# FNet mixing and a squared-ReLU FFN on one core: three of eight P-Q products of a block made on VectorE

## The chip, the cores and the metric

The kernel runs on one core of one Trainium2 chip. The metric is the device time of one execution in microseconds. The engines are named as in the profile: PE is TensorE's matmul stream and PEld its weight loads, DVE is VectorE, ACT is ScalarE, POOL is GpSimd, SP is SyncE, which here only issues transfers.

## The reference

The input x is 8 x 3008 x 256. It is Fourier-transformed along the sequence and along the features; the real part goes through a feed-forward layer without biases.

```python
X = np.fft.fft(x, axis=1)
X = np.fft.fft(X, axis=2)
h = np.maximum(X.real.reshape(24064, 256) @ w_in, 0.0)   # w_in 256 x 2048
out = (h * h @ w_out).astype(np.float32)                 # w_out 2048 x 256
```

## The kernel before, in words

**The algebra.** The real part at frequency k is a cosine product plus a sine product, and at -k it is the same cosine product minus the sine product. So only half of the frequencies are carried. For each of them the kernel holds two vectors over features, zc and zs, as fp16 columns with the features on the partitions. The feature transform is folded into the first weight: gh (three versions of w_in, 128 folded features by 2048) has the cosine weight in gh[0], the sine weight in gh[1], and in gh[2] minus two times the sine weight. Row 0 of zs is an exception: it carries the Nyquist feature, which has the same sign at k and -k, and row 0 of gh[2] is therefore zero. With P = gh[0]·zc and Q = gh[1]·zs the hidden value at k is P+Q, and at -k it is P-Q but for the Nyquist term, which stays.

**The units.** For each of the 8 batches VectorE folds x into sums and differences (`fold_steps`, L312 on: `d_even`, `n_cos`, `d_odd`, `n_sin`, `odds`, `nyq`, `even`), and PE multiplies the folded data with cosine and sine tables in two units per batch (`z_steps`). A unit has 12 or 18 matmuls of 376 or 377 columns into a PSUM tile pz. ACT copies the first half's product to es (L408) and the whole sum to zc or zs (L412); VectorE makes the mirrored columns as 2·es - pz (`minus`, L419). `d_odd` also issues the loads of the next batch's x on POOL (`load_x`, one direct and two indexed transfers, L118 and L123).

**The blocks.** All 12040 columns of zc and zs are cut into 25 windows, which the change's title calls blocks: 240, 512, 512, 240, then twenty of 512, and a last one of 296. A window has eight steps (`NST`), each for 256 of the 2048 hidden features, in a PSUM tile ph of two banks, one bank for each half (a = 0, 1) of 128 features. There are two such tiles (`ps_h`). A step does, in the order written:

- `pq(s)`: four matmuls, P+Q for the two halves (L570, L571);
- `square(s, 0)`: ACT's relu of both halves from PSUM to fp16 (L580), and VectorE's square of that into h2 (L582);
- `others(s)`: a share of the other work: fold jobs, two jobs of the second GEMM of the window before (sixteen matmuls of 256 columns, L500; in every second step also ACT's copy of the result, L506, and SP's stores, L482), and a share of the z matmuls for the next window;
- `turn(s)`: two matmuls with gh[2] on the same banks (L576), which turn P+Q into P-Q;
- `square(s, 1)`: relu and square again, columns reversed, into the second half of h2.

Every engine executes its instructions in the order in which the program writes them, and the framework inserts the waits. The folds of a batch are placed in one window, two ahead of the window in which the batch's first unit begins: one job in each of steps 0 to 4, `nyq` in step 5, `even` in step 6 (`fold_at`, `fold_jobs`). The z jobs of a unit are spread over the eight steps of the window ahead of the one in which its first column lies; the last job of the cosine half, with its L412 and L419, falls into step 5, that of the sine half into step 7.

Of the kernel before, what the change touches and what calls it, by code (L numbers as in the profile page):

```python
# [8 lines left out]
F32 = mybir.dt.float32  # L9
F16 = mybir.dt.float16  # L10
I32 = mybir.dt.int32
AF = mybir.ActivationFunctionType
ALU = mybir.AluOpType

HS = 32.0
P = 128
# [3 lines left out]
def rev_dim(ap, i):  # L20

    dims = [list(d) for d in ap.ap]
    step, cnt = dims[i]
    dims[i] = [-step, cnt]
    return bass.AP(tensor=ap.tensor, offset=ap.offset + step * (cnt - 1), ap=dims)
# [3 lines left out]
def kernel(  # L29
# [12 lines left out]
    nc = tc.nc  # L42
# [7 lines left out]
    NFC = F // P  # L50
    WN = 512
# [7 lines left out]
    NE = 2 * (E // 2) + 1  # L59
# [7 lines left out]
    wins = []  # L67
    g = 0
    while g < TOT:
        n = min(FIRST[len(wins)] if len(wins) < len(FIRST) else WN, TOT - g)  # L70
        wins.append((g, n))
        g += n
    NW = len(wins)

    def win_of(col):
        return max(w for w in range(NW) if wins[w][0] <= col) if col < TOT else NW
# [5 lines left out]
    col_of = {}  # L82
# [11 lines left out]
    const = ctx.enter_context(tc.tile_pool(name="const", bufs=1))  # L94
    tmp = ctx.enter_context(tc.tile_pool(name="tmp", bufs=2))
# [7 lines left out]
    ps_h = ctx.enter_context(tc.tile_pool(name="ps_h", bufs=2, space=bass.MemoryType.PSUM))  # L103
    ps_o = ctx.enter_context(tc.tile_pool(name="ps_o", bufs=2, space=bass.MemoryType.PSUM))
# [66 lines left out]
    def small(shape, name):  # L171
        return const.tile(shape, F32, name=name)
# [95 lines left out]
    dvec = small([P, 2], "dvec")  # L268
# [5 lines left out]
    at = const.tile([P, 2, P + 1], F32, name="at")  # L274
# [85 lines left out]

    gh = const.tile([P, 3, F], F16, name="gh")

    def gh_step(cc):
        f0 = cc * 512
        pg = ps_h.tile([P, 2, 512], F32, name="pg", tag="psh")
        for i, t in enumerate((c_all, s_n)):
            for c in range(2):
                nc.tensor.matmul(pg[:, i, :], t[:, c, 0:P], w16[:, c, f0 : f0 + 512], start=(c == 0), stop=(c == 1))  # L368
        nc.scalar.activation(gh[:, 0:2, f0 : f0 + 512], pg, AF.Copy, bias=0.0, scale=1.0 / HS)  # L369
# [7 lines left out]
    def zwin(w):  # L377
        if w not in zc:
            zc[w] = zp.tile([P, WN], F16, name="zc", tag="zc")
            zs[w] = zp.tile([P, WN], F16, name="zs", tag="zs")  # L380
        return zc[w], zs[w]
# [64 lines left out]
    run(*z0(0, 0))  # L446
    run(f0s["d_odd"])
    gh_step(0)
    run(*z0(0, 1))
    run(f0s["n_sin"], lambda: f0s["odd"](1), f0s["nyq"])  # L450
    gh_step(1)
    gh_step(2)
    run(*z0(1, 0))
    run(*z0(1, 1))
# [31 lines left out]
    def ffn2_steps(w, h2):  # L486

        g0, wn = wins[w]
        groups = [(q, min(P, 2 * wn - q)) for q in range(0, 2 * wn, P)]
        jobs = []  # L490
        st = {}

        def part(i, hf):
            q, m = groups[i]
            j = i % 2
            if j == 0 and hf == 0:
                st["po"] = ps_o.tile([P, 512], F32, name="po", tag="po")
            po = st["po"]
            for fc in range(hf * 8, hf * 8 + 8):
                nc.tensor.matmul(po[0:m, j * D : (j + 1) * D], h2[:, fc, q : q + m], wout16[:, fc, :], start=(fc == 0), stop=(fc == NFC - 1))  # L500
            if hf == 1 and (j == 1 or i + 1 == len(groups)):
                osb = osp.tile([P, 2, D], F32, name="osb", tag="osb")
                for a, b in ((i - j, i),) if j == 0 or m == P else ((i - 1, i - 1), (i, i)):
                    mm = groups[b][1]
                    lo, hi = (a % 2) * D, (b % 2 + 1) * D
                    nc.scalar.activation(osb[0:mm].rearrange("p s d -> p (s d)")[:, lo:hi], po[0:mm, lo:hi], AF.Copy, bias=0.0, scale=HS * HS)  # L506
                for b in range(i - j, i + 1):
                    q1, m1 = groups[b]
                    nu = max(0, min(m1, wn - q1))
                    if nu:  # L510
                        store(osb[:, b % 2, :], 0, g0 + q1, nu, False)
                    if nu < m1:
                        store(osb[:, b % 2, :], nu, g0 + 2 * wn - q1 - m1, m1 - nu, True)

        for i in range(len(groups)):
            for hf in range(2):
                jobs.append(lambda i=i, hf=hf: part(i, hf))
        return jobs

    def spread(jobs, i, n):  # L520
        return jobs[len(jobs) * i // n : len(jobs) * (i + 1) // n]

    def fold_jobs(i):
        f = fold_steps(i)
        return [f["d_even"], f["n_cos"], f["d_odd"], f["n_sin"], f["odds"], f["nyq"], f["even"]]

    fold_at = {}
    for i in range(2, B):
        fold_at[win_of(col_of[i, 0]) - 2] = i
    NST = NFC // 2  # L530
    old = None
    for w in range(NW):
        g0, wn = wins[w]
        h2 = h2p.tile([P, NFC, 2 * WN], F16, name="h2", tag="h2")
        zcw, zsw = zwin(w)

        lo = 0
        at = [[] for _ in range(NST)]
        post = [[] for _ in range(NST)]
        if w == 0:  # L540
            at[2] = [f0s["even"]]
        elif w == 1:
            fj = fold_jobs(1)
            at = [[f] for f in fj[0:5]] + [[], fj[6:7], []]
            post[5] = fj[5:6]
            lo = 6
        elif w == 2:
            te = table_steps(1)
            at = [[lambda: te["freq"](), lambda: te["args"](0)], [], [lambda: te["turns"](0)], [], [lambda: te["mods"](0)],
                  [lambda: te["absm"](0)], [lambda: te["sins"](0)], [lambda: te["coss"](0)]]  # L550
        elif w == 3:
            at = [[lambda: te["args"](1)], [lambda: te["turns"](1)], [lambda: te["mods"](1)],
                  [lambda: te["absm"](1), lambda: te["sins"](1)], [lambda: te["coss"](1)], [lambda: te["weigh"]()], [], []]
            lo = 6
        elif w in fold_at:
            fj = fold_jobs(fold_at[w])
            at = [[f] for f in fj[0:5]] + [[], fj[6:7], []]
            post[5] = fj[5:6]
        zj, zl = [], []
        for u in need[w + 1]:  # L560
            zu = z_steps(u)
            zj += [(zu, 0, 0), (zu, 1, 0), (zu, 0, 1), (zu, 1, 1)]
        f2 = ffn2_steps(*old) if old else []
        phs = {}

        def pq(s):
            ph = phs[s] = ps_h.tile([P, 2, 512], F32, name="ph", tag="psh")
            for a in range(2):
                f0 = (2 * s + a) * P
                nc.tensor.matmul(ph[:, a, 0:wn], gh[:, 0, f0 : f0 + P], zcw[:, 0:wn], start=True, stop=False)  # L570
                nc.tensor.matmul(ph[:, a, 0:wn], gh[:, 1, f0 : f0 + P], zsw[:, 0:wn], start=False, stop=True)  # L571

        def turn(s):
            for a in range(2):
                f0 = (2 * s + a) * P
                nc.tensor.matmul(phs[s][:, a, 0:wn], gh[:, 2, f0 : f0 + P], zsw[:, 0:wn], start=False, stop=True, skip_group_check=True)  # L576

        def square(s, sg):
            h1 = h1p.tile([P, 2, 512], F16, name="h1", tag="h1")
            nc.scalar.activation(h1[:, :, 0:wn], phs[s][:, :, 0:wn], AF.Relu)  # L580
            hv = rev_dim(h1[:, :, 0:wn], 2) if sg else h1[:, :, 0:wn]
            nc.vector.tensor_tensor(h2[:, 2 * s : 2 * s + 2, sg * wn : (sg + 1) * wn], hv, hv, op=ALU.mult)  # L582

        def others(s):
            for j in at[s]:
                j()
            for j in spread(f2, s, NST):
                j()
            for j in post[s]:
                j()  # L590
            if s == lo:
                zl[:] = [j for zu, part, h in zj for j in zu(part, h)]
            if s >= lo:
                for j in spread(zl, s - lo, NST - lo):
                    j()

        ng = 2 if w == 0 else 1
        for s0 in range(0, NST, ng):
            ss = range(s0, s0 + ng)
            for s in ss:  # L600
                pq(s)
            for s in ss:
                square(s, 0)
            for s in ss:
                others(s)
            for s in ss:
                turn(s)
            for s in ss:
                square(s, 1)
        old = (w, h2)  # L610
    for j in ffn2_steps(*old):
        j()
# [30 lines left out]
```

## Time and profile before

| what | value |
|---|---|
| median of 3 runs | 650.95 us (650.9 to 651.0) |
| the profiled execution's own time | 650.93 us |
| its span in the profile | 649.2 us |
| granted TensorE clock | 1.0 |
| ACT relu, 128 x 1024 | 352, mean 1026 ns |
| DVE square, 128 x 1024 | 352, mean 692 ns |
| PE matmuls of L576 with 512 columns | 352, mean 379 ns |
| DVE busy in eight stretches of 22 to 27 us in the middle | 10.3 to 17.7 us |

The profile is of one execution. The time of the execution is the span and 1.7 us around it, so sums are made against 650.93. A matmul's duration runs from its start to its modelled end, and matmuls overlap: 379 ns is the life of one, while the next starts 0.215 us later. Likewise two neighbouring instructions of ACT or DVE overlap by about 0.1 us, so the sum of the busy times is a little more than the time taken.

### The profile page before, as it was taken

Reading aid. Unit: us, or ns where it says so; the run is one execution under the profiler, and the core shown is the slowest. Engines: PE = TensorE matmul, PEld = TensorE weight load, DVE = VectorE, ACT = ScalarE, POOL = GpSimd, SP = SyncE. Lnnn points to the kernel's source line nnn. Section 1 sums busy time; section 2 is a strip of 40 time slices with the busy share of each in tenths; the row PEclk is TensorE's granted clock in tenths of the full one; section 3 lists DMA queues with packets and bytes.
Section 4 is the critical chain, followed back from the end, with each engine's and each line's share of the span. In section 5 each row is a group of like instructions: output and inputs, shape, how many; then the busy total and the mean of one; then the engine's idle time right before and its main releaser. Section 6 shows DMA issues by size and latency. Waiting matters only on the chain.

```text
span 649.2 us, 11358 instructions
## 1 busy us (share of the span) xinstructions
PE 628.7 (97%) x4524; PEld 442.1 (68%) x4524; DVE 359.9 (55%) x580; ACT 462.4 (71%) x616; POOL 38.1 (6%) x59
## 2 busy tenths in 40 slices
PE   3789999999999999999999999999999999999997
PEld 1456786667677666776667676766767667766786
DVE  8786566744475445644466454764547544444431
ACT  7877867776777777677667777777766777677662
POOL 6120000200010000100002000020000000000000
PEclk9999999999999999999999999999999999999999
DMA  8924120611152111611116111171111111111112
GB/s 161 163 43 102 33 66 18 129 49 28 42 114 77 33 50 33 124 57 50 33 49 130 42 41 48 36 135 45 49 34 49 33 49 35 41 41 46 38 49 71
DMA packets 34085, 40.06 MB, mean 62 GB/s; under 512 B 3568, under 2 KB 29680, under 8 KB 34032
## 3 DMA queue, kind: packets, MB, share of 16 engines
q1 hardware_dynamic: 27136, 24.65, 13.1%
q0 software_dynamic: 6896, 14.69, 13.0%
q8 instruction: 35, 0.57, 0.4%
q14 instruction: 18, 0.15, 0.1%
HBM read 29.37 MB, written 24.64 MB: 83 GB/s over the span
## 4 chain that ended last, share of the span: by engine, by line
PE 91%; ACT 4%; DMA 2%; issue 2%; DVE 1%; POOL 1%; ACTq 0%; POOLq 0%
PE po L500 49%; PE ph L571 12%; PE ph L576 12%; PE ph L570 12%; PE pz L403 5%; ACT h L580 2%; DMA w<-in_moe_w_in_dram 2%; ACT gh L369 1%; ACT osb L506 0%; POOL xo L123 0%; ACT zs L412 0%; PE pg L368 0%; DVE h L582 0%; DVE zs L419 0%; ACT cos L252 0%
## 5 line engine op out<-in xcount | busy, mean ns | idle before, releaser
L580 ACT ACTIVATE h<-ph 128x1024 f16<-128x1024 f32 (+2 forms) x400 | 368.9, 975 | 107.6 <-PE ph L576 104.7
L582 DVE TENSOR_TENSOR h<-h 128x1024 f16<-128x1024 f16 (+2 forms) x400 | 262.7, 660 | 247.1 <-ACT h L580 245.3
L500 PE MATMUL po<-wout,h 128*128 128x256 f16 (+1 forms) x3024 | 361.7, 273 | 0.0
L500 PEld LDWEIGHTS <-h 128*128 128x128 f16 (+1 forms) x3024 | 296.5, 98 | 71.5
L570 PE MATMUL ph<-zc,gh 128*128 128x512 f16 (+2 forms) x400 | 145.2, 366 | 1.2 <-ACT gh L369 0.7
L571 PE MATMUL ph<-zs,gh 128*128 128x512 f16 (+2 forms) x400 | 145.2, 366 | 1.1 <-DVE zs L419 0.9
L576 PE MATMUL ph<-zs,gh 128*128 128x512 f16 (+2 forms) x400 | 113.8, 366 | 3.2 <-ACT h L580 2.9
L506 ACT ACTIVATE osb<-po 128x512 f32<-128x512 f32 (+3 forms) x97 | 56.6, 587 | 67.0 <-PE po L500 63.6
L571 PEld LDWEIGHTS <-gh 128*128 128x128 f16 x400 | 39.0, 98 | 45.0 <-issue 2.8
L570 PEld LDWEIGHTS <-gh 128*128 128x128 f16 x400 | 39.0, 97 | 44.8 <-issue 3.7
L576 PEld LDWEIGHTS <-gh 128*128 128x128 f16 x400 | 39.0, 98 | 20.4 <-issue 6.3
L118 POOL DMA_DIRECT2D xo<-in_x_dram x8 | 6.1, 761 | 272.0 <-DVE fo L331 272.0
L123 POOL DMA_INDIRECT xo<-in_x_dram,idx_r x15 | 18.4, 1224 | 4.5 <-issue 4.3
L408 ACT ACTIVATE es<-pz 128x376 f32<-128x376 f32 (+1 forms) x32 | 15.4, 482 | 4.0 <-PE pz L403 4.0
L419 DVE SCALAR_TENSOR_TENSOR zs<-es,pz 128x376 f16<-128x376 f32 (+22 forms) x27 | 9.5, 384 | 15.6 <-ACT zs L412 15.6
L419 DVE SCALAR_TENSOR_TENSOR zc<-es,pz 128x376 f16<-128x376 f32 (+22 forms) x27 | 9.5, 384 | 13.0 <-ACT zc L412 13.0
L327 DVE TENSOR_TENSOR fe<-xo 128x3072 f16<-128x3072 f16 x8 | 14.3, 1786 | 0.3
L331 DVE TENSOR_TENSOR fo<-xo 128x3072 f16<-128x3072 f16 x8 | 14.2, 1778 | 0.0
L297 PE MATMUL pw<-spc 128*128 128x384 f16 x28 | 6.3, 395 | 8.2 <-DVE spc L293 8.2
L403 PE MATMUL pz<-cos,od 128*128 128x376 f16 x48 | 12.2, 323 | 1.8 <-DVE od L343 1.8
L403 PE MATMUL pz<-sin,od 128*128 128x376 f16 x48 | 12.2, 322 | 1.1 <-ACT es L408 1.1
L403 PEld LDWEIGHTS <-od 128*128 128x128 f16 x96 | 9.3, 98 | 5.5 <-DVE od L343 2.1
(88 smaller groups left out, 174.3 us busy)
## 6 DMA issues: line engine op xcount, KB each, us to landing
out_dram<-osb SPq DMA_DIRECT2D x93, 128.0 KB
xo<-in_x_dram POOLq DMA_DIRECT2D x7, 768.0 KB, 7.5
w<-in_moe_w_in_dram POOLq DMA_DIRECT2D x1, 1024.0 KB, 12.0
wout<-in_moe_w_out_dram POOLq DMA_DIRECT2D x1, 1024.0 KB, 16.4
out_dram<-osb SPq DMA_DIRECT2D x5, 120.0 KB
out_dram<-osb SPq DMA_DIRECT2D x4, 115.0 KB
out_dram<-osb SPq DMA_DIRECT2D x5, 80.0 KB
xo<-in_x_dram POOLq DMA_DIRECT2D x1, 384.0 KB, 4.8
```

The lines of the kernel that those rows point to most:

```text
L123: nc.gpsimd.indirect_dma_start(out=flat(q), out_offset=None, in_=bass.AP(tensor=x.tensor, offset=0, ap=[[XW, B * S * D // XW], [1, XW]]), ...
L327: nc.vector.tensor_tensor(fef[:, :, 1:129], lo, hi, op=ALU.add)
L403: nc.tensor.matmul(ps[:, 0:n], lhs, tab, start=(h == 0 and k == 0), stop=last, skip_group_check=True)
L408: nc.scalar.activation(es[:, 0:n], ps[:, 0:n], AF.Copy, bias=0.0, scale=1.0)
L419: nc.vector.scalar_tensor_tensor(out=zwin(w)[part][:, o : o + cnt], in0=es[:, a : a + cnt], scalar=2.0, in1=ps[:, a : a + cnt], op0=ALU.mu ...
L500: nc.tensor.matmul(po[0:m, j * D : (j + 1) * D], h2[:, fc, q : q + m], wout16[:, fc, :], start=(fc == 0), stop=(fc == NFC - 1))
L506: nc.scalar.activation(osb[0:mm].rearrange("p s d -> p (s d)")[:, lo:hi], po[0:mm, lo:hi], AF.Copy, bias=0.0, scale=HS * HS)
L570: nc.tensor.matmul(ph[:, a, 0:wn], gh[:, 0, f0 : f0 + P], zcw[:, 0:wn], start=True, stop=False)
L571: nc.tensor.matmul(ph[:, a, 0:wn], gh[:, 1, f0 : f0 + P], zsw[:, 0:wn], start=False, stop=True)
L576: nc.tensor.matmul(phs[s][:, a, 0:wn], gh[:, 2, f0 : f0 + P], zsw[:, 0:wn], start=False, stop=True, skip_group_check=True)
L580: nc.scalar.activation(h1[:, :, 0:wn], phs[s][:, :, 0:wn], AF.Relu)
L582: nc.vector.tensor_tensor(h2[:, 2 * s : 2 * s + 2, sg * wn : (sg + 1) * wn], hv, hv, op=ALU.mult)
```

## The change

Blocks from number 5 on that are 512 columns wide get another order in their steps 2, 4 and 6 (`second_kind`). There the two matmuls of `turn` are not made. Instead:

- `first(s)` multiplies P alone; for each half VectorE makes P' = P + wny·zny into an fp32 tile in SBUF, where zny is row 0 of zs on all 128 partitions and wny the Nyquist weight of each hidden feature;
- after `others(s)`, `second(s)` adds Q to the same banks;
- ACT makes the relu of P+Q, VectorE makes 2P' - (P+Q) in fp16 (`minus`), and VectorE squares the first relu;
- the relu of the second value, by ACT in place in SBUF, and its square are put off (`later`) into the next step, behind that step's first relu and square.

In the plain steps of all blocks but the first the square of P-Q is also put off, behind the next step's P', where that step is a changed one. zny is made by one transfer on SP's queue at the start of each such block, which reads row 0 of zs 128 times. wny is made once, in block 3 (`wny_step`: one small VectorE operation, sixteen matmuls of one column, a copy). The folds of batches 3 to 7 are spread over three blocks, begin four ahead of the batch's first unit, and stand in steps 0, 1 and 7 alone. That gives 57 changed steps in 19 blocks.

```diff
+    def wny_step():
+        nc.vector.tensor_scalar(out=e0, in0=dvec[:, 0:1], scalar1=0.0, scalar2=None, op0=ALU.is_equal)
+        pn = ps_o.tile([P, 512], F32, name="pn", tag="po")
+        for fc in range(NFC):
+            nc.tensor.matmul(pn[:, fc : fc + 1], gh[:, 1, fc * P : (fc + 1) * P], e0, start=True, stop=True)
+        nc.vector.tensor_copy(wny, pn[:, 0:NFC])
...
-        fold_at[win_of(col_of[i, 0]) - 2] = i
+        w1 = win_of(col_of[i, 0])
+        if i == 2:
+            fold_at[w1 - 2] = (i, [(0, 0), (1, 1), (2, 2), (3, 3), (4, 4), (5, 5), (6, 6)])
+        else:
+            fold_at[w1 - 4] = (i, [(0, 0), (1, 7)])
+            fold_at[w1 - 3] = (i, [(2, 0), (3, 7)])
+            fold_at[w1 - 2] = (i, [(4, 0), (5, 1), (6, 7)])
+    def second_kind(w):
+        if w < 5 or wins[w][1] < WN:
+            return ()
+        return (2, 4, 6)
...
+        def first(s):
+            ph = phs[s] = ps_h.tile([P, 2, 512], F32, name="ph", tag="psh")
+            pt = tmp.tile([P, 3, NE], F32, name="pt", tag="tt")...
+            for a in range(2):
+                f0 = (2 * s + a) * P
+                nc.tensor.matmul(ph[:, a, 0:wn], gh[:, 0, f0 : f0 + P], zcw[:, 0:wn], start=True, stop=True)
+            for a in range(2):
+                nc.vector.scalar_tensor_tensor(out=pt[:, a, 0:wn], in0=zny[:, 0:wn], scalar=wny[:, 2 * s + a : 2 * s + a + 1], in1=ph[:, a, 0:wn], op0=ALU.mult, op1=ALU.add)
+            return pt
+        def second(s):
+            for a in range(2):
+                f0 = (2 * s + a) * P
+                nc.tensor.matmul(phs[s][:, a, 0:wn], gh[:, 1, f0 : f0 + P], zsw[:, 0:wn], start=False, stop=True, skip_group_check=True)
+        def minus(s, pt):
+            vv = tmp.tile([P, 3, NE], F32, name="vv", tag="tm")...
+            nc.vector.scalar_tensor_tensor(out=vv[:, :, 0:wn], in0=pt[:, :, 0:wn], scalar=2.0, in1=phs[s][:, :, 0:wn], op0=ALU.mult, op1=ALU.subtract)
+            return vv
+        def relu_v(vv, wn=wn):
+            nc.scalar.activation(vv[:, :, 0:wn], vv[:, :, 0:wn], AF.Relu)
...
+        kinds = second_kind(w)
+        if kinds:
+            zny = tmp.tile([P, NE], F32, name="zny", tag="kf")[:, 0 : WN // 2].bitcast(F16)
+            z1 = zsw[0:1, 0:wn]
+            nc.sync.dma_start(out=zny[:, 0:wn], in_=bass.AP(tensor=z1.tensor, offset=z1.offset, ap=[list(z1.ap[0]), [0, P], [1, wn]]))
...
+                if s in kinds:
+                    pt = first(s)
+                    while later:
+                        later.pop(0)()
+                    others(s)
+                    second(s)
+                    h1 = relu(s, 0)
+                    vv = minus(s, pt)
+                    square(s, 0, h1)
+                    later += [lambda vv=vv, f=relu_v: f(vv), lambda s=s, vv=vv, f=square: f(s, 1, vv)]
+                else:
+                    pq(s)
+                    square(s, 0, relu(s, 0))
+                    while later:
+                        later.pop(0)()
+                    others(s)
+                    turn(s)
+                    h1 = relu(s, 1)
+                    later.append(lambda s=s, h1=h1, f=square: f(s, 1, h1))
+                    if s + 1 not in kinds:
+                        later.pop(0)()
```

More of the change, by code (lines that the diff above doesn't have):

```diff
@@ L361 @@
     gh = const.tile([P, 3, F], F16, name="gh")
+    wny = small([P, NFC], "wny")
+    e0 = const.tile([P, 1], F16, name="e0")
+    def wny_step():
[4 more added lines that the diff above has]
+        nc.vector.tensor_copy(wny, pn[:, 0:NFC])
     def gh_step(cc):
@@ L525, in fold_jobs @@
         return [f["d_even"], f["n_cos"], f["d_odd"], f["n_sin"], f["odds"], f["nyq"], f["even"]]
+    NST = NFC // 2
     fold_at = {}
     for i in range(2, B):
-        fold_at[win_of(col_of[i, 0]) - 2] = i
-    NST = NFC // 2
+        w1 = win_of(col_of[i, 0])
[9 more added lines that the diff above has]
+        return (2, 4, 6)
+    folds = {}
+    later = []
     old = None
@@ L551 @@
         elif w == 3:
+            post[7] = [wny_step]
             at = [[lambda: te["args"](1)], [lambda: te["turns"](1)], [lambda: te["mods"](1)],
@@ L555 @@
         elif w in fold_at:
-            fj = fold_jobs(fold_at[w])
-            at = [[f] for f in fj[0:5]] + [[], fj[6:7], []]
-            post[5] = fj[5:6]
+            i, jobs = fold_at[w]
+            if i not in folds:
+                folds[i] = fold_jobs(i)
+            for j, st in jobs:
+                (post if j == 5 else at)[st].append(folds[i][j])
         zj, zl = [], []
@@ L576, in turn, with relu, square @@
                 nc.tensor.matmul(phs[s][:, a, 0:wn], gh[:, 2, f0 : f0 + P], zsw[:, 0:wn], start=False, stop=True, skip_group_check=True)
-        def square(s, sg):
+        def relu(s, sg):
             h1 = h1p.tile([P, 2, 512], F16, name="h1", tag="h1")
             nc.scalar.activation(h1[:, :, 0:wn], phs[s][:, :, 0:wn], AF.Relu)
+            return h1
+        def square(s, sg, h1, wn=wn, h2=h2):
             hv = rev_dim(h1[:, :, 0:wn], 2) if sg else h1[:, :, 0:wn]
             nc.vector.tensor_tensor(h2[:, 2 * s : 2 * s + 2, sg * wn : (sg + 1) * wn], hv, hv, op=ALU.mult)
+        def first(s):
+            ph = phs[s] = ps_h.tile([P, 2, 512], F32, name="ph", tag="psh")
+            pt = tmp.tile([P, 3, NE], F32, name="pt", tag="tt").rearrange("p a n -> p (a n)")[:, 0 : 2 * WN].rearrange("p (a n) -> p a n", a=2)
+            for a in range(2):
[9 more added lines that the diff above has]
+        def minus(s, pt):
+            vv = tmp.tile([P, 3, NE], F32, name="vv", tag="tm").rearrange("p a n -> p (a n)")[:, 0:WN].bitcast(F16).rearrange("p (a n) -> p a n", a=2)
+            nc.vector.scalar_tensor_tensor(out=vv[:, :, 0:wn], in0=pt[:, :, 0:wn], scalar=2.0, in1=phs[s][:, :, 0:wn], op0=ALU.mult, op1=ALU.subtract)
+            return vv
+        def relu_v(vv, wn=wn):
+            nc.scalar.activation(vv[:, :, 0:wn], vv[:, :, 0:wn], AF.Relu)
         def others(s):
@@ L595, in others @@
                     j()
[L597 to L609, printed above, removed]
+        kinds = second_kind(w)
[3 more added lines that the diff above has]
+            nc.sync.dma_start(out=zny[:, 0:wn], in_=bass.AP(tensor=z1.tensor, offset=z1.offset, ap=[list(z1.ap[0]), [0, P], [1, wn]]))
+        if w == 0:
+            for s0 in range(0, NST, 2):
+                ss = (s0, s0 + 1)
+                for s in ss:
+                    pq(s)
+                for s in ss:
+                    square(s, 0, relu(s, 0))
+                for s in ss:
+                    others(s)
+                for s in ss:
+                    turn(s)
+                for s in ss:
+                    square(s, 1, relu(s, 1))
+        else:
+            for s in range(NST):
+                if s in kinds:
[8 more added lines that the diff above has]
+                    later += [lambda vv=vv, f=relu_v: f(vv), lambda s=s, vv=vv, f=square: f(s, 1, vv)]
+                else:
+                    pq(s)
+                    square(s, 0, relu(s, 0))
+                    while later:
+                        later.pop(0)()
+                    others(s)
+                    turn(s)
+                    h1 = relu(s, 1)
+                    later.append(lambda s=s, h1=h1, f=square: f(s, 1, h1))
+                    if s + 1 not in kinds:
+                        later.pop(0)()
+            if w + 1 == NW:
+                while later:
+                    later.pop(0)()
         old = (w, h2)
```

## The prediction

> **What bounds the kernel now.** I read three parts of the page first: busy time, chain of work, groups.
>
> ```profile
> PE 628.7 (97%) x4524; PEld 442.1 (68%) x4524; DVE 359.9 (55%) x580; ACT 462.4 (71%) x616; POOL 38.1 (6%) x59
> ...
> PE 91%; ACT 4%; DMA 2%; issue 2%; DVE 1%; POOL 1%; ACTq 0%; POOLq 0%
> ```
>
> PE carries 91% of the chain that ended last. A busy PE is not yet a full PE, since matmuls overlap, so the chain in order of time was read inside one block (start us, us, what):
>
> ```profile
> 306.98 1.75 PE po L500 x16
> 308.72 0.43 PE ph L576 x2
> 309.15 0.22 PE ph L570
> 309.37 0.22 PE ph L571
> 309.59 0.22 PE ph L570
> 309.80 0.22 PE ph L571
> 310.02 1.75 PE po L500 x16
> 311.76 0.43 PE ph L576 x2
> ```
>
> This is one whole step without a gap: 308.72 to 311.76 is 3.04 us, six matmuls of 512 columns at 0.215 and the second GEMM's sixteen at 1.75. The granted clock is 1.0 in every stretch I asked for. A 512-column matmul taken out of a step is therefore worth 0.215 us, as long as nothing else becomes late. What is late next is read from the waits (total, times, longest) and from the groups kept apart by shape (busy, mean ns, idle before):
>
> ```profile
> ACT h L580 <- PE ph L576: 104.7, 96, 1.4
> ...
> DVE zs L419 <- ACT zs L412: 15.6, 15, 3.0
> DVE zc L419 <- ACT zc L412: 13.0, 15, 1.5
> ...
> PE ph L576 <- ACT h L580: 2.9, 11, 0.4
> ```
>
> ```profile
> L580 ACT ACTIVATE h<-ph 128x1024 f16<-128x1024 f32 x352 | 342.3, 1026 | 101.6 <-PE ph L576 99.2 <-PE ph L571 2.1
> ...
> L582 DVE TENSOR_TENSOR h<-h 128x1024 f16<-128x1024 f16 x352 | 243.0, 692 | 226.0 <-ACT h L580 225.4
> ...
> L240 DVE SCALAR_TENSOR_TENSOR m<-kf,nvec,t 128x376 f32<-128x376 f32 x6 | 3.3, 606 | 0.1
> ...
> L419 DVE SCALAR_TENSOR_TENSOR zs<-es,pz 128x376 f16<-128x376 f32 x5 | 2.7, 548 | 6.3 <-ACT zs L412 6.3
> ...
> L246 ACT ACTIVATE sin<-m 128x1128 f16<-128x1128 f32 x2 | 2.3, 1144 | 0.7 <-DVE m L240 0.7
> ```
>
> The reader is to see that PE hardly waits for anyone (2.9 us for ACT in all), and that L419, whose inputs es and pz were complete long before, waits 30 times for an ACT instruction that only shares the PSUM bank it reads. Two readers of one bank run one after the other here, in the order written.
>
> **What is removed.** Full blocks from 5 to 23 are 19; three steps of each lose the two matmuls of L576: 114 x 0.215 = **24.5 us** of PE.
>
> **What is added to VectorE**, in each of 57 steps: two operations of 512 columns (P' from P, with a pointer scalar) and one of 1024 (2P' minus the bank). None is in the trace; the forms are. L419 at 290 columns takes 457 ns and at 376 547, so 1.05 ns a column: 512 columns are 688 ns and 1024 are 1.22 us. L240, the same operation with a pointer scalar, takes 606 at 376, 59 more, so the first two are 0.747 each. (From below: 0.688, if the pointer costs nothing; from above 0.9, the growth of L240 in proportion to columns.) Neighbouring VectorE instructions overlap: three of L240 take 1.65 together, so they start 0.52 apart at 0.606 each, 0.085 less. Squares start 0.605 apart (two in 1.28, the next 1.2 after the first). A pair of one changed and one plain step then needs 2 x 0.66 + 1.14 + 4 x 0.605 = 4.9 us of VectorE against PE's 2 x 3.04 - 0.43 = 5.65. Throughput fits. VectorE's busy time grows by 57 x 2.7 = 155, to some 515 us.
>
> **The relu that reads SBUF** instead of PSUM: ACT's 1128 columns from SBUF take 1144 at 0.838 ns a column (relu: 480 in 570, 1024 in 1026), so 1024 are 1.06. Nothing on its own: ACT is idle a quarter of the time.
>
> **The new loop, which sets the price.** In a changed step the product Q may not go into the bank before VectorE has read P out of it, and VectorE comes to that only after the previous changed step's work. From the second Q matmul of step 2 to that of step 4 (or 4 to 6): 0.45 until ACT starts (L576's second matmul to the relu after it), 1.03 relu, 0.02 to VectorE, which by the L419 rows waits for this relu as it reads the same banks; then VectorE in order: 1.14 subtraction, the square of P+Q, the next step's first square, the square of P-Q (3 x 0.605; the relu before the last one ends just in time), 0.66 and 0.75 for the next P'; 0.05 back to PE. Sum **5.91**, against 5.65 of PE work in a pair: PE waits 0.26. A block has two such links, so 0.52 where the block computes no z.
>
> 12 of the 19 blocks compute a unit of z. There the first link has 0.47 to 0.78 more PE work (three to five matmuls at 0.157) and its wait vanishes. The second is lengthened: the z subtraction L419 falls in step 5, between the last square and P', and its ACT copy stands behind the late relu and the copy of the outputs: 2.75 after the start of the link the relu, +0.97, +0.50, +0.52, then VectorE 0.55, 0.66, 0.75, 0.05: 6.75 against 5.65 + 0.47 to 0.63. It waits about 0.55. In all 7 x 0.52 + 12 x 0.55 = **10.2 us** given back. The first changed step has no such link: its P' can start when P is done, 6.5 us into the block, and ends at 8.0; PE wants the bank at 8.5.
>
> **Edits at one answer.** The 16 one-column matmuls for the Nyquist weights, once: the py pair's instructions start 0.03 apart, a weight load takes 0.098, so 0.5 to 1.6 us; I take **1.0**. The folds lie on VectorE in steps 7, 0 and 1, three plain steps of 9.1 us with six squares (3.7) and at most 2.7 of fold: covered, and the cost without cover would be the excess over some 5 us. With the odd fold its three loads of x move too, on POOL's own queue: the tightest is batch 3, issued 112.9 to 117.8, landing at most 10.1 later, 128; wanted from about 131. Nothing. The deferred squares are read one block later: nothing.
>
> **The broadcast of the Nyquist row (SP's queue).** It stands behind the last two stores of the block before (0.41 each) and needs the block's last zs: about 2.2 us into the block by the same kind of count. The first P' waits for it, and behind that on VectorE the previous square and the whole link. It must land before 7.0 us in a block without z, 7.7 in one with z: about 5.2 us after issue. No row shows a transfer that reads one partition 128 times. From below: the last store, same queue, issued at 646.1 and drained at 648.3, 2.2; a one-row load of x lands in 2.7. From above: 10.1, the slowest gather. Nearest by size and queue are the first two; I take 2.7, so nothing, and keep the other end as a rival.
>
> A rule speaks against this. The Trainium skill, "SBUF — State Buffer", section "Door 1: The DMA port swizzle", gives one port, to which a partition belongs, some 27 GB/s, and the next section a fixed 2 us; by that page the 128 KB from one partition would be an estimated 4.8 + 2 = 6.8 us, 1.6 late in each of 19 blocks, and the sum 30 us more. No run here shows it.
>
> **Sum** against the profiled execution (650.93; its span 649.2 and 1.7 around it; the median is 650.95): 650.93 - 24.5 + 10.2 + 1.0 = **637.6, say 638**. Unknowns of 0.15 on 38 links make 632 to 644.
>
> **Rivals.**
> - *The loop is shorter than counted* (the subtraction does not wait for the relu, or P' costs less): for it, that L419's wait may come from its output and not from the bank; against it, that the outputs are different columns. Then 1 us of the loop goes, little waits, 629 (626 to 632).
> - *VectorE is the bound*: P' at 0.9, and waits between engines dearer than 0.05. Each 0.1 on a link costs up to 3.8; 0.3 more gives 649. For it: the loop leaves VectorE almost no pause; against it: 4.9 of 5.65.
> - *The broadcast lands late*, the slower side. Place: the first P' of each block; every microsecond beyond 5.2 costs 19. It eats the gain of 13 at 5.9 us after issue. At 7.0, the median of the direct loads, 1.8 x 19 = 34: 672; at 6.2, 657. For it: all loads of x but the one-row one need 4.8 to 10.1; against it: those move 384 KB and more, this 128.
> - *The change doesn't do what it says* (Q of both halves waits for both P', as if the tile were one): 0.215 on each of 38 links more, 646.
>
> **Chances.** 638 as summed 0.46; short loop 0.14; VectorE bound or whole-tile waits 0.10 (of it 0.04 faster, 0.04 same, 0.02 slower); late broadcast 0.30 (0.02 same, 0.28 slower). Faster by over 0.2% (1.3 us, about what a measurement of this kernel can tell) 0.64, within 0.06, slower 0.30. The range of 628 to 660 leaves out part of the short loop (0.05) and the late broadcast beyond 6.3 us (0.14). The likeliest case alone is 632 to 644.
>
> **What would show it.** L576's successor count down by 114; in the waits, a new PE wait for VectorE's P' of about 10 us in 31 places; the subtraction waiting for ACT's relu; P' at about 0.75, subtraction at 1.22. If instead VectorE waits for a DMA ahead of the first P' for tens of us, the broadcast is late and I am wrong. If PE waits for nobody, the loop was counted too long.

## The result and the profile after

The changed kernel takes 686.34 us (684.44 to 687.01, 4 runs) against 650.92: the ratio is 1.054, with a 95% interval of 1.052 to 1.056. It is slower by 35.4 us, where 638 was forecast; 660 was the upper end of the range. The profiled execution took 684.44, its span is 682.6.

First the page of the changed kernel: busy time and groups (line numbers are the new ones; L605 is the old turn, L630 the late Q, L624 the two P', L634 the subtraction, L638 the relu from SBUF).

```profile
PE 617.4 (90%) x4426; PEld 432.7 (63%) x4426; DVE 483.6 (71%) x753; ACT 463.9 (68%) x616; POOL 37.8 (6%) x59
...
L634 DVE SCALAR_TENSOR_TENSOR vv<-pt,ph 128x1024 f16<-128x1024 f32 x57 | 69.6, 1221 | 70.5 <-ACT h L609 70.5
L624 DVE SCALAR_TENSOR_TENSOR pt<-zny,wny,ph 128x512 f32<-128x512 f16 x114 | 80.0, 743 | 53.1 <-DMA zny<-zs 50.3
...
L638 ACT ACTIVATE vv<-vv 128x1024 f16<-128x1024 f16 x57 | 60.2, 1057 | 20.1 <-DVE vv L634 20.1
L630 PE MATMUL ph<-zs,gh 128*128 128x512 f16 x114 | 34.7, 386 | 36.6 <-DVE pt L624 36.6
```

The three new operations last 743, 1221 and 1057 ns; 747, 1220 and 1060 were worked out. The subtraction waits for ACT's relu all 57 times. So the parts were priced rightly. What went wrong is PE's share, 90% instead of 97%, and the list of what PE waits for (total us, times, longest):

```profile
PE ph L630 <- DVE pt L624: 36.6, 41, 8.0
...
PE ph L600 <- ACT zs L422: 5.1, 9, 0.6
PE ph L600 <- DVE zs L429: 4.3, 4, 1.5
```

Behind the first line stand two different waits. They come apart in the timeline of block 12 (start us, us, engine and line, idle before). Here SP issues the broadcast, and the first P' starts 6.49 us later; for the last 1.58 of them VectorE idles until it lands:

```profile
325.10 0.49 SPq L657 DMA_DIRECT2D zny<-zs  x1
...
331.59 1.41 DVE L624 SCALAR_TENSOR_TENSOR pt<-zny,wny,ph 128x512 f32<-128x512 f16 x2 [1.58 <-DMA zny<-zs]
...
333.05 0.59 PE L630 MATMUL ph<-zs,gh 128*128 128x512 f16 x2 [0.53 <-DVE pt L624]
```

From issue to first use it is 6.4 to 8.7 us in the 18 blocks that waited, median 7.0. The worst is block 7, which began at 181.9 and whose broadcast SP issued only at 186.55, behind its stores; PE stood 8.02 us. Its stores ran late from 159.31 on, when one of the block before occupied SP for 13.6 us:

```profile
159.31 13.60 SPq L492 DMA_DIRECT2D out_dram<-osb  x1
```

The broadcast did not make this delay: in the run below that has no changed step and no broadcast the same store holds SP for 9.99 us (from 158.46). Both kernels issue three loads of x just before it, from 155.5 to 158.1; the kernel before issues them from 186.2 to 188.6, and there the same store takes 2.98. So the moved folds probably help to make block 7 late; what holds the store is not shown.

Over the trace these first waits of a block are 26.0 us in 17 places. The idle time shown begins at the modelled end of the matmul before, 0.16 after the next could have started, so the loss is 26.0 + 17 x 0.16 = 28.7.

The other 24 waits in that line, 10.6 us, are the loop of steps 4 and 6: 10.6 + 24 x 0.16 = 14.4 against the 10.2 forecast. One row of it:

```profile
337.69 1.40 DVE L624 SCALAR_TENSOR_TENSOR pt<-zny,wny,ph 128x512 f32<-128x512 f16 x2
...
339.14 0.59 PE L630 MATMUL ph<-zs,gh 128*128 128x512 f16 x2 [0.28 <-DVE pt L624]
```

Both Q matmuls start after the second P' has ended (337.69 + 1.40 = 339.09), the first too: Q of one half waits for both halves, 0.215 more per link than summed. With it the sums become 0.48 for a link without z and 0.77 for the late one with z; the trace has 0.44 to 0.49 and 0.62 to 0.85 (the hidden 0.16 included), so apart from this term the loop was counted right.

The two lines of L600 I had not on the list at all. At the start of a block the first sine matmul reads zs, and zs is now late:

```profile
322.59 1.06 ACT L638 ACTIVATE vv<-vv 128x1024 f16<-128x1024 f16 x1 [0.37 <-DVE vv L634]
...
323.39 0.38 PE L599 MATMUL ph<-zc,gh 128*128 128x512 f16 x1
...
323.55 0.58 ACT L516 ACTIVATE osb<-po 128x512 f32<-128x512 f32 x1
...
324.03 0.54 ACT L422 ACTIVATE zs<-pz 128x92 f16<-128x92 f32 x2
...
324.32 0.38 PE L600 MATMUL ph<-zs,gh 128*128 128x512 f16 x1 [0.55 <-ACT zs L422]
```

In step 7 ACT does step 6's late relu, then the output copy, then the last copy of zs, and PE wants that copy at 323.61. It cost 9.4 us in 13 places, 11.5 with the hidden 0.16; before the change it was 0.9 in 3.

The balance: 650.9 - 24.5 (matmuls gone) + 0.4 (Nyquist weights) + 28.7 + 14.4 + 10.1 (block starts, less those of before) = 680.0 against 684.4. The other 4.4 stands beside a lowered clock. Stretches of 5 us at two of the long waits (length, busy of PE, PEld, DVE, ACT and POOL, granted clock, share of the DMA engines, GB/s):

```profile
160.00:165.00 5.00, 3.41 (x12) 1.70 (x12) 3.67 (x5) 2.03 (x3) 0.00 (x0) 0.70 1.03 182
...
190.00:195.00 5.00, 0.00 (x0) 0.00 (x0) 0.46 (x1) 0.00 (x0) 0.00 (x0) 0.77 0.64 62
195.00:200.00 5.00, 4.01 (x16) 1.97 (x16) 3.45 (x6) 2.28 (x3) 0.00 (x0) 0.55 0.06 20
```

From 190 to 195 PE does nothing, it waits; after the wait its matmuls of 512 columns start 0.43 us apart instead of 0.215:

```profile
196.80 0.63 PE L599 MATMUL ph<-zc,gh 128*128 128x512 f16 x1
197.23 0.63 PE L600 MATMUL ph<-zs,gh 128*128 128x512 f16 x1
```

The same is seen from 162.0 to 165.4, behind a wait of 2.44, and from 578.9 to 581.8, behind one of 2.85. With the 3.5 us up to 199.5 that is 9.8 us of PE's work at half speed, a loss of about 4.9 by this estimate, which fits the 4.4.

### The profile page after: what moved, and what is told of

Same layout as the page of the kernel before. It is cut to its first block, busy times and chain, and to the rows that moved or that the text cites. A ratio compares the mean times of both kernels' runs of the same rounds, so it can differ in the third digit from the quotient of the medians.

```text
span 682.6 us, 11392 instructions
## 1 busy us (share of the span) xinstructions
PE 617.4 (90%) x4426; PEld 432.7 (63%) x4426; DVE 483.6 (71%) x753; ACT 463.9 (68%) x616; POOL 37.8 (6%) x59
## 5 line engine op out<-in xcount | busy, mean ns | idle before, releaser
L609 ACT ACTIVATE h<-ph 128x1024 f16<-128x1024 f32 (+2 forms) x343 | 316.9, 964 | 157.0 <-PE ph L630 66.2
L614 DVE TENSOR_TENSOR h<-h 128x1024 f16<-128x1024 f16 (+2 forms) x343 | 216.2, 650 | 52.9 <-ACT h L609 49.4
L634 DVE SCALAR_TENSOR_TENSOR vv<-pt,ph 128x1024 f16<-128x1024 f32 x57 | 69.6, 1221 | 70.5 <-ACT h L609 70.5
L624 DVE SCALAR_TENSOR_TENSOR pt<-zny,wny,ph 128x512 f32<-128x512 f16 x114 | 80.0, 743 | 53.1 <-DMA zny<-zs 50.3
L600 PE MATMUL ph<-zs,gh 128*128 128x512 f16 (+2 forms) x286 | 103.4, 366 | 9.6 <-ACT zs L422 5.1
L599 PE MATMUL ph<-zc,gh 128*128 128x512 f16 (+2 forms) x286 | 103.4, 366 | 1.2 <-ACT gh L379 0.7
L605 PE MATMUL ph<-zs,gh 128*128 128x512 f16 (+2 forms) x286 | 79.9, 361 | 3.4 <-ACT h L609 3.0
L638 ACT ACTIVATE vv<-vv 128x1024 f16<-128x1024 f16 x57 | 60.2, 1057 | 20.1 <-DVE vv L634 20.1
L630 PE MATMUL ph<-zs,gh 128*128 128x512 f16 x114 | 34.7, 386 | 36.6 <-DVE pt L624 36.6
L600 PEld LDWEIGHTS <-gh 128*128 128x128 f16 x286 | 28.1, 98 | 32.4 <-issue 4.2
L630 PEld LDWEIGHTS <-gh 128*128 128x128 f16 x114 | 11.1, 97 | 47.4 <-issue 44.9
L614 DVE TENSOR_TENSOR h<-vv 128x1024 f16<-128x1024 f16 x57 | 39.5, 693 | 0.7 <-ACT vv L638 0.7
L605 PEld LDWEIGHTS <-gh 128*128 128x128 f16 x286 | 27.9, 97 | 16.7 <-issue 6.6
L622 PE MATMUL ph<-zc,gh 128*128 128x512 f16 x114 | 33.9, 379 | 0.0
L622 PEld LDWEIGHTS <-gh 128*128 128x128 f16 x114 | 11.1, 98 | 13.5
```

The costliest lines, as they stand in the source:

```text
L624: nc.vector.scalar_tensor_tensor(out=pt[:, a, 0:wn], in0=zny[:, 0:wn], scalar=wny[:, 2 * s + a : 2 * s + a + 1], in1=ph[:, a, 0:wn], op0=A ...
L630: nc.tensor.matmul(phs[s][:, a, 0:wn], gh[:, 1, f0 : f0 + P], zsw[:, 0:wn], start=False, stop=True, skip_group_check=True)
L634: nc.vector.scalar_tensor_tensor(out=vv[:, :, 0:wn], in0=pt[:, :, 0:wn], scalar=2.0, in1=phs[s][:, :, 0:wn], op0=ALU.mult, op1=ALU.subtract)
L638: nc.scalar.activation(vv[:, :, 0:wn], vv[:, :, 0:wn], AF.Relu)
```

## The experiments

Theory A: the broadcast is late because one partition is its only source. Rival B: it is late because it stands behind the stores on SP's queue. Rival C: the loop of the changed steps, not the broadcast, is the loss.

**Own rows.** The Nyquist row is left out; the transfer has the same size, queue and waits.

```diff
-nc.sync.dma_start(out=zny[:, 0:wn], in_=bass.AP(tensor=z1.tensor, offset=z1.offset, ap=[list(z1.ap[0]), [0, P], [1, wn]]))
+nc.sync.dma_start(out=zny[:, 0:wn], in_=zsw[:, 0:wn])
```

> The broadcast is replaced by a transfer of the same 128 KB on the same queue, with the same waits, that reads each partition's own row of zs; the Nyquist row is so left out of the second kind of product (other values are added in its place). Theory A, one partition as the only source is what makes the transfer slow: it lands 2 to 3.5 us after issue instead of 6.4 to 8.6, the wait of the first P' for the DMA (50.3 us) goes below 10, PE's 28.7 us behind it and some 5 us of lowered clock go, 651 to 654 us. Rival B, the transfer stands behind the stores on its queue: landing and time stay, 683 to 687. Rival C, the loop between changed steps is what costs: the DMA wait may go but the time stays above 670.

660.91 us, one run. VectorE waits for the transfer in 2 blocks instead of 18. One of them is block 7, where it lands late again:

```profile
182.47 1.15 SPq L657 DMA_DIRECT2D zny<-zs  x1
...
189.52 1.40 DVE L624 SCALAR_TENSOR_TENSOR pt<-zny,wny,ph 128x512 f32<-128x512 f16 x2 [8.31 <-DMA zny<-zs]
```

7.05 us with 128 source partitions: there the single source is not the cause, and stores stand ahead on the queue. So A holds for most blocks and B for some. C falls as the only cause. The time stayed 7 us above A's figure, and the wait of PE in block 7 alone is 6.7.

**POOL's queue**, one partition as in the change.

```diff
-nc.sync.dma_start(out=zny[:, 0:wn], in_=...)
+nc.gpsimd.dma_start(out=zny[:, 0:wn], in_=...)
```

> The same broadcast from one partition, issued by POOL instead of SP, so that no store stands ahead of it. Theory A: landing stays at 6 to 8 us; the blocks in which SP issued it late (4.7 us into block 7) gain, 672 to 686 us. Rival B: landing falls to 2 to 4 us, 651 to 660 us. Rival C: above 670 whatever the landing.

662.49 us, one run, below A's figure by 10 and above B's. For POOL the profile gives the landing: 6.2 / 7.3 / 13.1 us (least, median, most). The transfer is as slow as on SP; it is only issued earlier (block 6: 151.22 instead of 152.05) and has no stores ahead. In six blocks (7, 10, 13, 16, 19 and 22) zs is complete a block earlier, and POOL then issues the broadcast 15 to 33 us before the first P'. Block 7:

```profile
159.14 0.61 POOL L657 DMA_DIRECT2D zny<-zs  x1
...
183.48 0.75 DVE L624 SCALAR_TENSOR_TENSOR pt<-zny,wny,ph 128x512 f32<-128x512 f16 x1 [1.01 <-PE ph L622]
```

On SP's queue the same transfers came behind the stores of the block before, and these six blocks made 15.7 of the 26.0 us of first waits. PE's waits for P' fall from 36.6 to 19.3.

**POOL's queue and own rows**, both edits together.

> As the run on POOL's queue, but every partition reads its own row of zs (the Nyquist row is so left out of the second kind of product). The profile gives the landing of POOL's transfers, which it does not for SP's. If the single source partition is what makes the transfer slow: 1.8 to 3.5 us from issue to landing against 6.2 to 13.1 (median 7.3) with the same queue and one partition, and 655 to 657 us. If the size or the queue does it: landing above 5.5, and 660 to 664 us.

652.14 us, one run, 3 below the least that was expected. These are the transfer's landings in this run:

```profile
DMA to landing us min/median/max: 2.1/3.5/9.0
```

and with one source partition on the same queue:

```profile
DMA to landing us min/median/max: 6.2/7.3/13.1
```

Same queue, same 128 KB, same producers; only the number of source partitions differs. The profile gives the landing of 10 transfers with one source and of 15 with 128; in the eight blocks that have both, the one source lands later every time, by 1.0 to 5.3 us. Nor do only a few DMA engines work for it: from 190 to 195 in the changed kernel, the row shown above, all 16 are busy for 0.64 of the time on average at 62 GB/s, where 175 to 180 of the same trace has 0.20 at 64. The one source costs 4.1 us at the least values, by estimate 128 KB at 32 GB/s, and 662.49 - 652.14 = 10.3 us of time. No first P' waits for the transfer any more, and nothing is left over: 650.9 - 24.5 + 0.4 + 15.3 of loop (11.1 in 26 places) + 10.1 of block starts = 652.2. The broadcast's price is therefore 686.34 - 652.14 = 34.2 us, and it has two causes that overlap: with POOL's queue first it falls by 23.9 and with own rows then by 10.3; with own rows first by 25.4 and with POOL's queue then by 8.8. Either alone takes most of it, since a transfer that is late by a little only costs what goes beyond the threshold. Some 5 of the 34.2, by the estimate above, is the clock, 0.999 here against 0.99.

**No changed step.** The folds, the Nyquist weights and the new program order alone.

```diff
-        return (2, 4, 6)
+        return ()
```

> No step is of the second kind; the folds over three blocks, the Nyquist weights and the changed program order stay. All theories that put the loss into the changed steps: 650.5 to 652.5 us (650.9 and up to 1.6 for the Nyquist weights). If the moved folds and the loads of x cost something themselves: above 653.

651.27 us against 650.91: the moved folds cost nothing that can be told, as predicted.

**Broadcast by PE.** No transfer; one matmul with a row of ones and a copy by ACT in step 0.

```diff
-            nc.sync.dma_start(out=zny[:, 0:wn], in_=...)
...
                     square(s, 0, relu(s, 0))
+                    if s == 0 and kinds:
+                        pb = ps_z.tile([P, 512], F32, name="pb", tag="pz")
+                        nc.tensor.matmul(pb[:, 0:wn], one, z1, start=True, stop=True)
+                        nc.scalar.activation(zny[:, 0:wn], pb[:, 0:wn], AF.Copy, bias=0.0, scale=1.0)
```

> The broadcast is made by one PE matmul with a row of ones (0.215 us a block) and one ACT copy of 512 columns (0.6) in step 0; no DMA. Theories A and B alike: the first P' waits for nothing, 28.7 us of PE waits and some 5 of clock go, 4.1 us of matmul come, 653 to 658 us. Rival C: above 670.

659.91 us (ratio 1.013, 1.011 to 1.015), 2 above the range expected: the matmul costs more than 0.215 (below). PE's waits for P' are 11.1 us in 26 places, those of L600 9.4 in 13. Even without the transfer the changed kernel is slower than the one before, so two more causes were tested on top of this kernel. In all these kernels the lines stand two or three further down: L632 or L633 is the late Q, L626 or L627 the P', L602 or L603 the sine matmul.

**The loop.** The square of the second kind is put behind the next changed step's P'.

```diff
                     pt = first(s)
+                    while hold:
+                        hold.pop(0)()
...
                     later += [lambda vv=vv, f=relu_v: f(vv), lambda s=s, vv=vv, f=square: f(s, 1, vv)]
+                    if s + 2 in kinds:
+                        hold.append(later.pop())
```

> On top of the broadcast by PE: the square of the second kind of a changed step is put behind the next changed step's P', which takes 0.605 out of the loop. Theory of the loop (5.91 counted and 0.215 more because Q of the first half waits for both P', against 5.65 of PE work): the loop falls to 5.52, PE's waits for P' fall from 26 to below 14, and some 13 us go: 645 to 649 us from 659.9. Rival, these waits are not on the path that sets the end (the PE time returns at the next block start): 657 to 660 us.

653.53 us (ratio 1.0039, 1.0029 to 1.0049): 6.4 us gone, half of what was expected. The lines of its waits:

```profile
DVE zc L431 <- ACT zc L424: 11.0, 14, 0.9
...
PE ph L633 <- DVE pt L627: 6.9, 12, 0.7
```

The 14 waits of the blocks without z are gone. The 12 left are the second links of the blocks with z: VectorE now comes earlier to the z subtraction, and waits there for ACT's zc copy (11.0 us; in the kernel above 3.6). In that link ACT's order sets the time, as the prediction's sum for it had it; the expectation for this run had counted the square into it too.

**Steps 1, 3 and 5.** No late relu stands in step 7, and the z subtraction of step 5 falls behind that step's P'.

```diff
-        return (2, 4, 6)
+        return (1, 3, 5)
...
-            fold_at[w1 - 4] = (i, [(0, 0), (1, 7)])
-            fold_at[w1 - 3] = (i, [(2, 0), (3, 7)])
-            fold_at[w1 - 2] = (i, [(4, 0), (5, 1), (6, 7)])
+            fold_at[w1 - 4] = (i, [(0, 6), (1, 7)])
+            fold_at[w1 - 3] = (i, [(2, 6), (3, 7)])
+            fold_at[w1 - 2] = (i, [(4, 6), (5, 7), (6, 7)])
```

> On top of the broadcast by PE: the changed steps are 1, 3 and 5 and the folds stand in steps 6 and 7, so that no late relu stands ahead of ACT's last copy of zs in step 7. Theory of the block start (ACT and VectorE finish zs late, the first Q matmul of the next block waits, 9.4 us of PE waits of which 0.9 were there before): these waits return to 1 to 2 us. The z subtraction also leaves the loop, so in the blocks with z the loop's waits go: 640 to 645 us. Rival, the waits move to another place: 655 to 660 us.

642.63 us (ratio 0.986, 0.984 to 0.988), faster than before. Its waits of PE:

```profile
PE ph L632 <- DVE pt L626: 4.6, 14, 0.3
...
PE ph L602 <- DVE zs L431: 1.2, 4, 0.5
```

The block start costs 1.2 us of waits, 0.9 before the change. The 14 waits left are the two links in each of the seven blocks without z, as the loop has it.

**Both.**

> Both edits on top of the broadcast by PE. If the three causes add up: 650.9 - 24.5 + 4.1 of broadcast matmuls + 0.4 for the Nyquist weights + 2 to 5 of rest, 633 to 637 us, faster than the kernel before. Rival, VectorE or ACT has become the bound, so that waits return elsewhere: 645 us or more.

635.22 us (635.02 to 635.35; ratio 0.975, 0.973 to 0.977). No wait for P' is left, and PE is back where it was:

```profile
PE 613.4 (97%) x4445; PEld 431.8 (68%) x4445; DVE 483.3 (76%) x754; ACT 475.4 (75%) x635; POOL 40.1 (6%) x59
...
PE 88%; ACT 4%; DVE 2%; DMA 2%; issue 2%; POOL 1%; ACTq 0%; POOLq 0%
```

The broadcast matmul's price is read in the timeline of this kernel:

```profile
300.90 0.38 PE L603 MATMUL ph<-zs,gh 128*128 128x512 f16 x1
301.21 0.38 PE L695 MATMUL pb<-zs,one 1*128 1x512 f16 x1
301.53 1.92 PE L512 MATMUL po<-wout,h 128*128 128x256 f16 x16
```

From 300.90 to 301.53 it is 0.63, of which the first matmul has 0.215: 0.41 for one row of 512 columns, the same in all 19 blocks, 7.9 together. Then 650.9 - 24.5 + 7.9 + 0.4 = 634.7 against 635.2. The idea of the change holds; its broadcast, its place in the block and the place of one square did not.

## Why the prediction was wrong, point by point

- **What bounds the kernel, and what a matmul is worth**: right. With every added wait taken away the time is within 0.5 us of the sum.
- **The new operations and their durations**: right to 4 ns. (The upper end for P', 0.9, was called L240 grown in proportion to columns; that is 0.83.) The folds and the Nyquist weights: right (0.36 measured, 1.0 said).
- **The broadcast**: the step that failed. It was put at 2.7 us from issue and so at nothing, by the last store and the one-row load as the nearest rows. Those were nearest by queue and by size, but neither reads one partition 128 times, and the profile said so little on that that the upper end, 10.1, should have weighed more. It takes 6.4 to 8.7 and costs 34 us. The point from which it is late was put at 5.2 us after issue; in the 16 blocks that show it (time to first use less PE's loss) it is 5.3 to 7.0, median 5.7. By that rival's own rule a landing at 7.0 makes 672, and the two terms below bring that to 686. That this is the measured time is in part luck: the rule's 34 stands for 28.7 of waits, 8.2 of them in block 7 alone, and some 5 of clock, which was not counted. The Trainium skill's "SBUF — State Buffer" gives 27 GB/s for one port in the section "Door 1: The DMA port swizzle"; with the fixed 2 us of its section "The DMA setup-cost knee" that is an estimate of 6.8. The least landing measured here from one partition, 6.2, is 0.6 below it. I gave the late broadcast 0.30, against rows that did not show the case.
- **The queue**: I counted two stores ahead, 0.41 each, and took zs to be complete only at the start of a block. In six blocks it is complete a block earlier, and SP's order kept the broadcast back. In block 7 SP issued the broadcast 4.7 us into the block, and with own rows it still took 7.05 there. On POOL's queue the same broadcast costs 10.3 instead of 34.2.
- **The loop**: mechanism right, 14.4 for 10.2. The term missing is the 0.215 by which Q of the first half waits for the second half's P'; it stood among the rivals at 646 instead of in the sum. The part with z was right too: ACT's copy is last there, as summed.
- **What is late at the start of a block**: not on the list, 10.1 us. I followed the late relu to the output copy and the broadcast, and did not ask who else waits behind it on ACT: the next block's first sine matmul.
- **The rivals**: the late broadcast was named with its place and price, and the range cut it off at 660, a landing of 6.3 us, which is less than any of the 18 first waits of the changed kernel show (6.4 at least). The loop of 629 is out: the subtraction waited for the relu 57 of 57 times, though their outputs are different tiles.

## What to carry to other kernels

A transfer that gates an in-order engine in every pass of a loop has to be priced by a row of its own kind, the number of source partitions included; where there is none, the far end of the range is the working value, and a broadcast through PE or another route is the safer form. It also belongs on a queue where nothing stands ahead that becomes ready later than its own input. When an instruction is put off into a later step, list everything that stands behind it on its engine until the end of the pass, and for each of them who reads it first. A loop between in-order engines is counted link by link with the waits as the framework places them, by whole tile and not by half.

## What the runs showed of the hardware

- One source partition: 128 KB to 128 partitions lands 6.2 us (least) and 7.3 (median) after issue, against 2.1 and 3.5 from 128 partitions, on the same queue (10 and 15 transfers).
- SP's issue itself can be held: in the changed kernel one store occupied SP's queue for 13.6 us (from 159.31) and a later one for 4.2 (179.89 to 184.09), and the broadcast behind them went out at 186.55.
- PE's clock falls beside long waits: the granted clock was 0.77 in the 5 us before the 8.02 us wait ended, 0.55 in the next 5, and then 1.0 again. Behind the waits of 2.44 and 2.85 us it fell as well, behind those of 2.00 and 2.26 it stayed at 1.0. In the kernel with both edits it stays at 1.0.
- A one-row matmul of 512 columns costs PE 0.41 us between two others, where one of 128 rows costs 0.215.
